# A new written order for the steps of chunk-selected attention and a gated feed-forward

## The chip, the core and the metric

The kernel runs on one core of a Trainium2 chip. Its engines are PE (matrix products), DVE (vector work), ACT (activation functions), POOL (simple tensor work, and issuing of DMAs) and SP (issuing of DMAs). Each takes its instructions from a queue of its own, strictly in the order written; they meet at semaphores. The metric is the device time of one execution in microseconds (us).

## The reference

There are 4 batches of 8 heads, with 768 positions and 64 channels per head. Attention is causal, and each query uses at most 6 key chunks of 32 positions: those with the highest upper bound of the score, which comes from each chunk's channel-wise minimum and maximum of the keys. A feed-forward follows on the 3072 x 512 result.

```python
k_min = np.min(k_chunks, axis=3); k_max = np.max(k_chunks, axis=3)
ub = sum(maximum(q * k_min, q * k_max))          # per query and chunk
top_chunks = np.argsort(where(causal, ub, -1e9))[..., -6:]
attn = softmax(where(sel & causal, scale * q @ k.T, -1e9)) @ v
xn = x / sqrt(mean(x * x) + 1e-6) * rms_g        # x: heads side by side
out = (silu(xn @ w_gate) * (xn @ w_val)) @ w_out # 512 -> 1536 -> 512
```

## The kernel before

**Tiling.** Two heads make a pair p, so there are 16 pairs, four for each batch b. A pair is prepared (place `a`), scored (place `s`) and feeds one column block of its batch's rows. The feed-forward of a batch goes in two halves of 384 rows (places `f0.0`, `f0.1`, ... ), each behind a norm (`n0.0`, ...) of three 128-row blocks.

**Steps of preparation.** kload and qload bring keys and queries by SP's queue. kT and qT turn them on PE (line 520, three 128 x 128 transposes a step), kE and qE copy them out of PSUM (helper line 290 on ACT, 294 on DVE). kmx and kmn reduce the chunks' extremes, dif subtracts them, relu takes the positive part of the queries (line 636 on ACT, 638 on DVE or POOL). ub multiplies bounds on PE (lines 737 and 795), ubE copies them out, up turns them, ubm adds the causal mask, max and sel find and mark the six best, grd guards, selT and selC (pairs 0 to 2) or a DMA transpose qX (line 560, from pair 3 on) put the marks below the queries. kC and qC cast keys and queries to bf16 (line 294 on POOL), qN lays queries out for the DMA transpose. The keys' operand, one of three sets in KE, also has constant rows: a step ke0 copies them into set 0, and two steps ke (70 and 71, lines 388 and 389, two DMAs each on SP's queue) into sets 1 and 2.

**Scores and the rest.** sc are the score products (line 882, with a causal triangle at 888 in batch 0), exp the exponentials on ACT (line 899), mask cuts the triangle on POOL in later batches (line 905), av multiplies by the values (line 918), xb divides and stores a head's columns (lines 938 and 939, DVE). The norm sums squares (sq: line 966 on ACT, 969 on DVE), eps (979), a root on POOL (987), scales rows (xs, line 995, DVE) and turns them (tp, line 1017 on PE, with an eviction tpE, in batch 0; DMA transposes xT in later batches). gate (line 1051) and val (line 1072) are four products of 384 columns each; tanh (1058, ACT), tg (1064) and hh (1080, both DVE) form the gated activation; po (line 1092) is the output product, poE its eviction, out the store (line 1107). The weights wg, wv (line 440) and wo (445) are loaded in two parts each by POOL's queue, which also loads v (line 476).

**What sets the order.** Nothing is scheduled at run time. Every unit of work is a step with a number, counted in the order in which the code adds it. PROGRAM is one long list of words: a letter for the engine (P PE, A ACT, D DVE, G POOL, S SP), the step's number, and the slots of the buffers that the step opens. `run` assigns them, and the steps are then emitted in that order, so the list fixes each engine's queue, which of two allowed engines does a step, and which slot of a pool (8 PSUM banks `ps`, 7 `nat` for loads, 3 `set`, ...) a buffer takes. A step that opens a slot waits for the last user of that slot.

```python
for word in program.split():
    n, _, slots = word[1:].partition(":")
    s = self.steps[int(n)]
    s.eng = engines[word[0]]
```

**Fillers.** Steps 4 to 51 and 290 to 328 (busy, line 339) multiply zeros into a bank that nobody reads. Only those that the list names are emitted.

**Numbers used below.** 70, 71: ke. 222, 330, 541, 470: the key loads of pairs 2, 3, 6, 5. 331, 333: pair 3's kT; 542, 544: pair 6's; 471, 473: pair 5's. 103, 239, 346, 415: relu of pairs 0, 2, 3, 4. 69: ke0. 199: the last score of pair 1 in the new list. 412: a cast of pair 4's keys; 343: one of pair 3's. 76 and 78: the two parts of wg; 77 and 79: of wv. 1260 to 1319: gates, vals and what belongs to them in `f0.0`; a gate is 1260 + 5 ht and its val three more, for the 12 blocks ht. 1335 to 1348: the second norm, with eps 1338, root 1339, xs 1340 and tp 1341.

## Time and profile before

| what | value |
|---|---|
| median of 3 runs | 312.37 us (311.37 to 313.6) |
| the profiled execution | 312.63 us |
| its span, first to last instruction | 310.9 us |
| PE, DVE, ACT, POOL busy | 300.8, 232.2, 182.2, 119.5 us |
| granted TensorE clock, mean | 0.999 |
| DMA moved | 35.35 MB |

The profile shows one execution. Busy times of PE include modelled ends of matmuls that overlap the next one; where it matters, starts are compared. "Idle before" names what ended a wait. The page's row of PE by 40 slices has 9 tenths or more in all but four slices: the first, third, seventh and last.

### The profile page before, as it was taken

The page shows a single profiled execution, that of the slowest core. Times are in us where ns is not written, and L with a number is a line of the kernel's source. Part 1 is how long each engine was busy: PE and PEld are TensorE (multiplying, and loading weights), DVE is VectorE, ACT ScalarE, POOL GpSimd, SP SyncE. Part 2 cuts the span into 40 slices and gives each one's busy share as a digit, 9 for nine tenths or more (in the row PEclk, how much of TensorE's full clock was granted, in tenths as well). Part 3 has the DMA queues.
Part 4 walks back from the last instruction along what each step waited for, and adds up shares of the span by engine and source line. Part 5 has one row for each costly group of instructions (what it writes and reads, how often), then busy time and mean ns, then how long its engine had stood idle before and what let it go on. Part 6 is the DMA issues. An engine that isn't in the chain of part 4 may idle for free.

```text
span 310.9 us, 7415 instructions
## 1 busy us (share of the span) xinstructions
PE 300.8 (97%) x2764; PEld 190.4 (61%) x2782; DVE 232.2 (75%) x651; ACT 182.2 (59%) x405; POOL 119.5 (38%) x176
## 2 busy tenths in 40 slices
PE   7989998999999999999999999999999999999995
PEld 3657875666667764667776456666665455565542
DVE  5888988998977887789987897875743764477621
ACT  5789987672588763866997336667872303433110
POOL 8588856654547840632775104514030110000000
PEclk9999999999999999999999999999999999999999
DMA  9999999999999997996237136533000055200013
GB/s 172 221 170 175 121 209 209 158 168 150 154 176 206 201 163 145 231 163 165 55 26 50 33 74 178 53 74 29 3 0 2 34 86 186 102 2 0 0 70 136
DMA packets 113300, 35.35 MB, mean 114 GB/s; under 512 B 106224, under 2 KB 110064, under 8 KB 113264
## 3 DMA queue, kind: packets, MB, share of 16 engines
q1 hardware_dynamic: 83152, 26.62, 43.0%
q0 software_dynamic: 28512, 7.87, 25.4%
q10 hardware_dynamic: 1600, 0.39, 0.6%
q8 instruction: 22, 0.36, 0.5%
q14 instruction: 14, 0.11, 0.1%
HBM read 28.57 MB, written 6.29 MB: 112 GB/s over the span
## 4 chain that ended last, share of the span: by engine, by line
PE 87%; DMA 8%; POOL 2%; ACT 1%; issue 1%; ACTq 0%; SPq 0%; POOLq 0%
PE vp L1072 20%; PE po L1092 20%; PE gp L1051 19%; PE sc L882 10%; PE av L918 6%; DMA wg<-in_moe_w_gate_dram 5%; PE pq L520 3%; PE pk L520 3%; PE ub L795 2%; DMA knat<-in_k_dram 2%; PE ub L737 1%; DMA qnat<-in_q_dram 1%; POOL ke L294 1%; PE up L817 1%; PE busy L339 1%; POOL rt L638 1%
## 5 line engine op out<-in xcount | busy, mean ns | idle before, releaser
L899 ACT ACTIVATE pt<-sc 128x512 bf16<-128x512 f32 (+1 forms) x192 | 94.0, 556 | 21.2 <-PE sc L882 18.4
L1058 ACT ACTIVATE sg<-gp 128x384 bf16<-128x384 f32 x96 | 45.7, 495 | 72.2 <-PE gp L1051 62.6
L1072 PE MATMUL vp<-xT,wv 128*128 128x384 bf16 x384 | 74.4, 326 | 1.6 <-DMA wv<-in_moe_w_val_dram 1.5
L1051 PE MATMUL gp<-xT,wg 128*128 128x384 bf16 x384 | 74.2, 326 | 0.1
L1092 PE MATMUL po<-wo,hh 128*128 128x512 bf16 x271 | 66.8, 379 | 0.7
L1064 DVE SCALAR_TENSOR_TENSOR tg<-sg,gp 128x384 bf16<-128x384 bf16 x96 | 51.9, 549 | 20.6 <-ACT sg L1058 19.2
L1080 DVE TENSOR_TENSOR hh<-vp,tg 128x384 bf16<-128x384 f32 x96 | 51.5, 552 | 18.5 <-PE vp L1072 17.7
L882 PE MATMUL sc<-qs,ke 128*128 128x128 bf16 (+4 forms) x420 | 59.3, 251 | 0.0
L1072 PEld LDWEIGHTS <-wv 128*128 128x128 bf16 x384 | 35.8, 98 | 26.4 <-DMA wv<-in_moe_w_val_dram 1.8
L1051 PEld LDWEIGHTS <-wg 128*128 128x128 bf16 x384 | 35.7, 98 | 22.5 <-DMA wg<-in_moe_w_gate_dram 0.5
L1092 PEld LDWEIGHTS <-hh 128*128 128x128 bf16 x288 | 27.5, 98 | 27.5
L918 PEld LDWEIGHTS <-pt 128*128 128x128 bf16 x672 | 34.8, 98 | 11.1 <-POOL pt L905 0.3
L918 PE MATMUL av<-vx,pt 128*128 128x65 bf16 x672 | 41.2, 193 | 0.1
L905 POOL TENSOR_SCALAR_AFFINE_SELECT pt<-pt 128x512 bf16<-128x512 bf16 (+1 forms) x48 | 24.5, 522 | 38.5 <-ACT pt L899 38.1
L882 PEld LDWEIGHTS <-ke 89*128 89x128 bf16 (+1 forms) x420 | 31.0, 97 | 10.0 <-issue 1.4
L294 POOL CAST ke<-kt 64x768 bf16<-64x768 f32 x30 | 25.3, 846 | 7.3 <-PE sc L882 2.8
L987 POOL TENSOR_TENSOR ri<-ms,mhalf 128x3 f32<-128x3 f32 x8 | 7.2, 904 | 33.6 <-DVE ms L979 33.5
L995 DVE SCALAR_TENSOR_TENSOR xs<-xb,ri,gains 128x512 bf16<-128x512 bf16 x24 | 17.2, 751 | 3.1 <-POOL ri L987 2.9
L939 DVE TENSOR_TENSOR xb<-av,rden 128x384 bf16<-128x384 f32 (+1 forms) x34 | 18.2, 534 | 1.2
L520 PE MATMUL pk<-ident_f,knat 128*128 128x128 f32 x96 | 16.0, 282 | 1.7 <-DMA knat<-in_k_dram 1.7
L476 POOL DMA_DIRECT2D vx<-in_v_dram x16 | 17.3, 1079 | 0.1
L653 DVE MAX8 m<-ubm 128x8 f32<-128x8 f32 (+4 forms) x192 | 16.8, 160 | 0.2
(91 smaller groups left out, 300.6 us busy)
## 6 DMA issues: line engine op xcount, KB each, us to landing
out_dram<-osb SPq DMA_DIRECT2D x24, 256.0 KB, 2.3
knat<-in_k_dram SPq DMA_DIRECT2D x30, 192.0 KB, 4.4
qnat<-in_q_dram SPq DMA_DIRECT2D x30, 192.0 KB, 5.1
vx<-in_v_dram POOLq DMA_DIRECT2D x16, 192.0 KB, 5.9
wg<-in_moe_w_gate_dram POOLq DMA_DIRECT2D x2, 768.0 KB, 11.7
wv<-in_moe_w_val_dram POOLq DMA_DIRECT2D x2, 768.0 KB, 10.6
...
qs<-qn SPq DMA_TRANSPOSE x26, 2.8
```

What stands on the lines that cost most here:

```text
L294: engine[e].tensor_copy(out_, in_)
L520: nc.tensor.transpose(t[:, j * P:(j + 1) * P], nat[w].tile[:, j0 + j].rearrange("p h d -> p (h d)"), ident_f[:])
L882: nc.tensor.matmul(t[:, x:x + m, :].rearrange("p a b -> p (a b)"), ke[kk, kb * P:(kb + 1) * P], qs[kk, q0 * P:(q0 + m) * P], start=not tri ...
L899: nc.scalar.activation(out=t[:, 0:nn, :], in_=sc.tile[:, 0:nn, :], func=ACT.Exp, scale=SCALE)
L905: nc.gpsimd.affine_select(out=pt.tile[:, 0:nd, :], in_=pt.tile[:, 0:nd, :], compare_op=ALU.is_ge, fill=0.0, base=0, pattern=[[0, nd], [1, ...
L918: nc.tensor.matmul(av.tile[:, qi - i0, :], pt.tile[:, x, :], VX[c.v.slot][:, hl * NT + kb, :], start=(begin and m == 0), stop=(left[0] == ...
L1051: nc.tensor.matmul(t[:], wg[:, g, hs], XT[b].tile[:, g, cols], start=(g == 0), stop=(g == NP - 1))
L1058: nc.scalar.activation(out=t[:], in_=gp.tile[:], func=ACT.Tanh, scale=0.5)
L1064: nc.vector.scalar_tensor_tensor(out=t[:], in0=sg.tile[:], scalar=1.0, in1=gp.tile[:], op0=ALU.add, op1=ALU.mult)
L1072: nc.tensor.matmul(t[:], wv[:, g, hs], XT[b].tile[:, g, cols], start=(g == 0), stop=(g == NP - 1))
L1080: nc.vector.tensor_tensor(out=t[:], in0=vp.tile[:], in1=tg.tile[:], op=ALU.mult)
L1092: nc.tensor.matmul(po.tile[:], hhs[ht].tile[:, th * P:(th + 1) * P], wo[:, ht, :], start=(ht == 0), stop=(ht == NHT - 1))
```

## The change

Only PROGRAM differs. Each of the 1878 steps of the old list is in the new one; the new list has ten more words, fillers 30 to 39 (36 fillers instead of 26). 91 steps go to their other engine: 43 from DVE to ACT, 30 from ACT to DVE, 7 from POOL to ACT, 4 from DVE to POOL, 4 from POOL to DVE and 3 from ACT to POOL. Of the relus named above, 103 goes from DVE to ACT, 346 from POOL to ACT, 239 from ACT to DVE and 415 from POOL to DVE; ke0 goes from ACT to DVE. Nearly every step's place and slots change. On SP the q and k loads keep their order, but the two ke steps, the transposes and the stores move among them: 70 now stands ahead of 222, and 71 between 222 and 330. On POOL the loads of v and of the weights keep their order; the casts, differences, guards and masks move among them.

The beginning of both lists, to the first feed-forward steps, and their ends:

```diff
@@ PROGRAM @@
 PROGRAM = (
-    "S83:0 S88:1 S89 S82 D3 G0 D56 D55 D53 D54 D60 G63 A2 G65 P4:0 D59 P5:1 G66 P6:2 D58 P7:3 D57 G67 P8:4 S154:2 "
-    "P9:5 G68 P86:6 S159:3 P10:7 G72 A87:0 P11:0 A69 D97:0 P92:1 D96:0 P12:2 G64 S335:4 G73 P84:3 D93:1 P90:4 A85 "
-    "P13:5 P14:7 A91 P15:6 D95 P16:0 A99:0 P17:2 G101 D94 S222:5 P157:1 P155:5 D98 G62 A158:2 D103:3 P18:3 G61 "
-    "P19:7 P20:4 S71 D156 P104:6,0 G102 D1 D52 D165:1 G168:1 P160:2 S330:6 A106:0 P162:3 D164:1 G74 A105 P21:1 "
-    "A161:4 P107:7 A163 G167 P336:4 S70 D108:0 P338:5 A171:5 P22:0 G166 D109:2 P23:6 P24:1 A100 D110 S541:0 "
-    "P172:2,3 A337:6 D112:0 A339 D111 P225:7 A173:0 D174 P113:0 G346:3 A226:1 S227:1 P175:6 A114 P223:1 D176:1 "
-    "P25:4 P26:5 D177:3 P331:2 P333:3 D178 A224 G115:0 S404:2 P119:7 D332:2 A334 P147:6 A179:1 P135:4 D340:4 "
-    "A148:0 G170 P128:5 P116:0 A136:1 D180 S399:3 P544:1 A117:2 D341:2 P150:3 P125:2 A545:0 P181:6 P141:4 A151:3 "
-    "D232:5 A126:4 P138:0 G342 G236:2 P347:1,3 A120:5 D182 A129:6 G169 P228:2 A139:7 P230:7 S546:5 G183:1 D348:0 "
-    "A349 P542:5 D229:5 A231 P350:6 D233:3 A142:8 P190:0 G345:0 P118:1 P121 A239:6 P144:3 P149:2 D351:2 P152 "
-    "P184:7 G234 G235 A191:9 D352:6 P240:4,6 D543 A145:2 G238 D353 A185:5 P215:0 P122:5 G251:2 A241:0 D242 P143 "
-    "A216:0 P146 P131:3 P243:7 A354 P405:4 A123:3 G237 D244:0 P209:6 P140 P137 A132:8 P218:0 D245:7 P193:7 A210:2 "
-    "G358:3 P407:5 D406:3 A219:7 P203:3 A194:1 D246 P133 P124 P187:6 A408 D248:0 G247 P127 A204:8 P196:0 D153:0 "
-    "P402:4 A188:3 P199:7 P217:5 P249:3 D355 A197:4 P130 P212:2 D250 S356:0 P211 A403:4 P195:6 G556:1 P206:0 "
-    "A200:0 A213:6 P186 P400:4 G555:1 D134 A207:2 P264:7 P201 S357 P286:3 P214 P277:2 A265:1 G554 D401 P189 "
-    "P258:0 P252:1 A278:5 D409:0 G343 P274:7 A259:0 S475:6 P261:4 A253:6 P205 D552:0 P192 G344 P198 P255:2 A275:3 "
-    "P271:0 G415:1 D202 A256:8 S470:1 P267:1 P279:7 P220 P208 A287:9 A268:4 P266:2 D551:1 P283:6 A272:5 P288 "
-    "P362:3 P257 P276 A262:7 P280:1 S75 D221 P269 P254 P369:0 P260 A281:2 P359:4 G412:2 D410:1 A370:1 P263 P282 "
-    "A284:9 P273 P366:5 G76 D270 A363:8 P285 A360:3 P389:1 G77 P371:0 P364:6 P386:3 D329 A367:4 P361 P373:2 "
-    "A390:6 G411 D365 G553 P368 P395:4 G78 A387:0 P471:5 D372 P416:7,1 D472:6 A1248:2,0 D1246:1 A1247:2 P379:6 "
-    "P478:3 D418:0 A396:7 P547:0 D1249:3 D417 P27:5 A374:2 G1250:4 P397:1 D548:5 P392:4 P476:7 A380:5 P382:5 "
-    "P473:2 D1251:0 A383:9 P391 P388 P376:0 A393:1 D1254:1 P375:6 P384 P1252:5 A479:2 P394 D1257:2 P381 A477 "
-    "P1255:4 P419:3 A377:8 D398 G486:0 P1258:7 A1253:0 P378 D1259 P549:0 A1256 D385 P28:1 P29:5 A474 D420:1 "
-    "P1260:7 A1336:5,0 D421:7 G413 P1280:1 A1335:1 D480:6 P1268:4 A1337:2 G414:0 D422 A1261:0 P1285:6 D1338:0 "
-    "D423 A1281:1 D424 G1339:1 P1270:5 D1262:2 A1286:3 S426 D1282:4 P1275:2 A1271:5 D1346:3 P1263:3 A1276:6 S425 "
-    "D1272:7 P1265:7 D1277:0 P1305:1 D1343:0 A1266:1 S559:0 P1288:5 D550 D1264:0 P1344:2 G557:3 P1315:0 D1287:5 "
-    "A1345 S564:4 D1267:6 P439:3 A1316:2 P449:6 D1289:1 P445:2 P1300:7 A450:3 D1269:2 P1295:5 G427:0 A440:4 "
-    "D481:2 A1301:3 P1283:6 A446:7 D1317:1 G79 A1296:5 P457:4 D1302:6 P560:3 A458:6 P436:2 G482 D1297:2 P1347:0 "
-    "G81 A561:1 P562:7 D1348 P565:4 A563 D1284:3 P428:5 P463:3 A437:0 D1340:1 P432:0 G572:0 P487:7,6 A429:2 "
-    "D570:3 A464:9 P1273:2 G451 A489:0 D488 A566:4 P1341:5 G485:0 P567:3 A1306:3 D1342 P459:6 A433:1 P490:7 "
-    "D1274:4 G430 P1364:4 D569:2 G80 P466:5 P1349:0 A467:5 D491:0 P465 P442:2 D571 D568 P1399:5 A443:8 D1307:5 "
...
-    "S1848 P1935:1 D1894:4 S1843 D1924:7 P1851 D1919:15 P1926 D1852:0 P1936 S1853 P1931 P1937 P1932 D1938:2 P1927 "
-    "S1939 D1933:1 S1934 A1928:0 S1929 "
+    "S83:0 S88:1 S89 S82 G0 D3 D59 P4:0 P5:1 A2 G65 D55 D56 P6:2 D53 D1 D60 P7:3 G66 P8:4 D54 P9:5 G61 G67 S154:2 "
+    "P86:6 P10:7 G68 P11:0 S159:3 A87:0 G74 P12:1 D69 P13:2 P92:3 G64 G62 D96:0 G63 P90:4 G72 A93:1 S335:4 P14:5 "
+    "D97:0 P84:7 A91 P15:0 P16:6 D85 A103:2 P17:1 P18:2 S70 P19:5 D95 G99:0 A101 P155:3 D94 P157:4 S222:5 D52 D58 "
+    "P20:0 G98 G100 A158:3 P104:6,7 D57 A156 G73 D164:1 S71 P160:1 A106:0 P162:2 A105 D165:1 G102 P21:5 P107:0 "
+    "A163:4 P22:4 S330:6 A161 P338:3 D108:0 G166 P336:7 G168:1 A171:5 D109:2 P23:6 P24:5 D110 P25:2 G169 A337:6 "
+    "P172:4,1 A111:0 D112 G345:0 S541:1 P113:0 A174:0 P225:6 A173 D114 P223:5 A339 P175:2 A346:0 P26:7 S227:0 "
+    "P27:1 D176:1 P141:4 A226:2 P135:3 D177:3 A224 P331:0 D178 A136:0 P150:7 P333:1 G115:0 D332:1 P138:2 A151:1 "
+    "A179:1 P122:6 D180 A334 P128:5 P144:3 G170 A139:2 P28:7 D341:2 P181:0 A123:3 S404:2 P147:1 A129:4 P29:7 "
+    "G236:2 D340:4 P30:2 A182 P31:6 P32:7 P542:5 S399:3 G342 P33:2 G167 P347:6,7 D543:5 A142:5 D233:3 G235 A148:6 "
+    "P184:2 D232:5 A349:0 P196:0 A348 P215:5 G183:1 P34:4 A145:7 P35:1 P228:7 A185:8 S546:4 P230:6 G234 A197:9 "
+    "D229:4 P193:4 P350:1 D231 P140:3 P124:2 P143 P125:7 A194:2 D239:3 G237 P407:0 A216:3 D351:2 P240:6,4 D408:6 "
+    "A126:5 G414:1 D352:6 P209:1 P149 A242:0 D241 P119:5 A210:6 D353 G251:2 P243:0 P130 P131:7 P137 D244:0 P190:4 "
+    "A132:4 P187:6 A120:0 G354 D245:7 P146 P544:1 G238 A188:7 D246 P133 P195:0 P116:7 A191:4 P402:5 D248:0 G247 "
+    "P218:6 A117:2 D355 P206:4 A403:0 P192 G344:0 P249:7 A207:4 P118 S356 P127 P203:5 D250 A219:2 P212:4 G358:3 "
+    "P121 A204:5 P152 P400:6 D134:0 A213:0 P274:7 S357 P189 P405:5 D401 A275:1 P271:4 D406 A545 P277:2 P205:6 "
+    "A272:7 D153 P186 P214 P217 P286:7 P283:1 A278:5 P264:5 D415:2 P258:4 A284:8 P280:3 D410:0 P199:2 A287:0 "
+    "P273:1 S475:5 A200:3 G412:1 P198 P285 P261:7 A281:7 D552:1 P201 P288 P211 P252:2 G343 A259:9 P276 P255:3 "
+    "D551:0 A265:8 S470:6 P366:4 A262:3 P359:5 D409:1 A253:0 P282 P279 P386:7 S75 A367:6 D329 P260:2 P208 P220 "
+    "A256:1 P266 P369:4 G76 D202 A387:7 P379:1 P382:3 P257 A370:5 G411 D221 P362:7 G77 A360:9 P254 P263 P267:0 "
+    "P389:4 A268:4 P371:5 P368 A363:2 P392:6 G78 A390:8 P269 P373:0 D372 P395:7 A393:1 D270 P364:4 P361 P471:5 "
+    "A380:0 P549:6 D365 A383:3 P473:2 P478:1 A396:5 D1246:2,0 P376:4 A1248:1 P547:3 D1247:2 P476:7 A472:3 A377:6 "
+    "P397:5 D1249:3 P394 D548:4 G1250:4 A374:4 P378:4 A477:1 P416:3,0 D1251:0 D1257:1 P391 P384 P1252:7 A418:0 "
+    "P381 A417 P388 D1254:2 P1258:0 A1253:0 P375 P419:3 D398 A479 P1255:7 A1259 D385 P36:1 P37:5 A1256 D420:1 "
+    "P38:1 D550 A1335:5,0 P1280:0 D421:7 A1337:1 D1336:2 P1285:4 D422 P1275:5 A1286:0 D1338:6 D424 P1265:3 A423 "
+    "G1339:1 A1281:1 D1287:2 S426 A1276:3 P1270:1 D1282:4 A1266:5 P1288:7 D1340:3 A486:6 S425 P1260:6 D1343:0 "
+    "A1271:6 A474 P1341:4 D1346:1 P1263:0 A557:2 G483:2 D1272:7 P1268:2 A1342 D1267:0 S559:0 A1261:1 G413 P1344:1 "
+    "D1289:0 P1315:4 D1345 G484 P1305:3 D1277:6 A1316:5 S564:1 D1262:2 P1347:7 G554:0 P1300:1 D1317:3 A1348 "
+    "G556:0 D1269:1 P445:5 P457:6 A1306:1 P1283:4 D1264:2 A458:2 G553 G427:0 P463:7 A446:9 P428:2 D1284:3 P436:0 "
+    "P460:6 A429:5 D481:2 P560:5 G79 A461:1 P432:4 P1349:2 D1307:5 A437:6 G485:1 D480:2 P562:6 A561:0 P567:3 "
+    "A1301:0 P1273:0 A563 D568:3 G482 G430 A1350:2 P439:5 D1302:4 P487:6,3 A433:8 G555 D1274:4 D569:3 G434 P565:1 "
+    "A489:0 P1399:4 A566 D488 D570:3 P453:0 A440:3 P490:3 A454:0 P435:6 P431 P1295:1 D1351:1 A575:5 G571 G455 "
+    "D491:0 P449:5 G81 P459:0 A1296:0 D492:4 P577:2,3 A464:7 D493 A1400:7 D494 A450:4 D495 P456 P1278:7 A578:0 "
+    "S496 G451 A582 P39:5 G80 D1279:5 P583:2 D1297:2 P1379:3 S497 D1401:6 P441 P447 P579:5 D584:2 A1380:0 D585:1 "
+    "P1303:7 D581 D580 P438 P466:1 P442:4 D586:5 P1364:2 A467:8 D592:7 A443:5 G573:1 D1381:7 P1298:5 D1304:6 "
+    "G574:1 P1310:1 D1299:7 P1402:4 D593 A1311:0 P524:3 D594 D595 P503:7 P468 P1367:5 A525:2 D1403:8 S597 A504:0 "
+    "D1312:4 P452 P507:3 P520:4 A1365:2 P462 P528:7 A508:3 P1318:1 D1366:6 S596 A521:9 D587 P1290:3 A529:6 "
...
+    "D1869:10 P1898:5 P1935:6 D1899:13 D1838:17 P1844:4 D1909:19 P1925:1 P1845 P1903:5 P1930:7 D1904:21 P1846 "
+    "P1926 A1847:0 P1849:0 S1848 P1927 P1931 A1928:1 P1679 P1932 D1680:2 P1936 S1681 D1933:0 P1850 S1934 S1929 "
+    "P1841 P1937 D1842:2 P1851 S1843 A1938:0 S1939 A1852:1 S1853 "
 )
```

176 rows, old and new, of the table PROGRAM are left out of this document.

## The prediction

> **What bounds the kernel now.** I read the page's head first, then busy time by stretch, then the chain of waits.
>
> ```profile
> span 310.9 us, 7415 instructions
> PE 300.8 (97%) x2764; PEld 190.4 (61%) x2782; DVE 232.2 (75%) x651; ACT 182.2 (59%) x405; POOL 119.5 (38%) x176
> ```
> ```profile
> 0.00:17.60 17.60, 15.75 (x126) 9.20 (x128) 12.56 (x50) 11.97 (x22) 12.85 (x29) 1.00 1.10 198
> 17.60:49.00 31.40, 29.42 (x448) 22.71 (x447) 27.88 (x82) 28.74 (x68) 22.70 (x28) 1.00 1.29 169
> 49.00:62.00 13.00, 11.48 (x79) 7.02 (x78) 11.43 (x34) 8.83 (x22) 8.41 (x9) 1.00 1.17 178
> 62.00:180.00 118.00, 117.58 (x1201) 78.21 (x1208) 99.92 (x282) 78.09 (x178) 58.49 (x87) 1.00 0.91 139
> 180.00:300.00 120.00, 119.58 (x887) 70.18 (x893) 76.83 (x202) 54.02 (x117) 17.06 (x26) 1.00 0.24 52
> ```
> ```profile
> 56.87 0.65 PE vp L1072 x4
> 301.31 5.79 PE po L1092 x26
> 307.13 0.60 ACT osb L292
> ```
>
> A row of the second fence gives the stretch, its length, and busy us with counts for PE, PEld, DVE, ACT and POOL, then the granted clock, DMA share and GB/s. From 62 to 300 PE is idle 118.00 - 117.58 + 120.00 - 119.58 = 0.84 us. Nothing is to be won there unless work is taken away, and an order takes none away. The end is PE's last product at 301.31 + 5.79 = 307.10, one eviction of 0.60 and the last store, and both orders end so. A new order can win before 62, and can lose anywhere.
>
> Busy time flatters PE there, since ends are modelled. I use starts instead: four 384-column products take 0.65 us on the chain.
>
> ```profile
> 16.96 0.84 PE L520 MATMUL pk<-ident_f,knat 128*128 128x128 f32 x6
> 20.75 0.52 PE L520 MATMUL pk<-ident_f,knat 128*128 128x128 f32 x3 [1.28 <-DMA knat<-in_k_dram]
> 42.09 0.52 PE L520 MATMUL pk<-ident_f,knat 128*128 128x128 f32 x3 [0.42 <-DMA knat<-in_k_dram]
> 48.51 0.59 PE L339 MATMUL busy<-zeros 128*128 128x512 bf16 x2
> 48.99 1.46 PE L1051 MATMUL gp<-xT,wg 128*128 128x384 bf16 x8
> 51.90 0.82 PE L1072 MATMUL vp<-xT,wv 128*128 128x384 bf16 x4 [1.45 <-DMA wv<-in_moe_w_val_dram]
> ```
>
> This is PE's timeline; brackets hold idle time and what ended it. The first gate starts at 48.99. Ahead of it stand 140 PE steps that compute, in the old order and, counted in the program, in the new one: the same 140. After it the same steps remain too. So the forecast is a shift of the first gate, plus what changes in the waits after it.
>
> **The change, part by part.** Loads first.
>
> ```profile
> 8.57 1.72 SPq L500 DMA_DIRECT2D knat<-in_k_dram  x2
> 10.40 0.79 SPq L388 DMA_DIRECT2D ke<-e_all  x1
> 11.24 0.59 SPq L389 DMA_DIRECT2D ke<-e_all  x1
> 11.88 1.27 SPq L500 DMA_DIRECT2D knat<-in_k_dram  x2
> 13.19 0.55 SPq L388 DMA_DIRECT2D ke<-e_all  x1
> 14.48 1.23 SPq L500 DMA_DIRECT2D knat<-in_k_dram  x2
> ```
> ```profile
> knat<-in_k_dram SPq DMA_DIRECT2D x30, 192.0 KB, 4.4
> ```
>
> SP issues pair 2's keys at 8.57, a set's constant rows (ke, two DMAs) at 10.40, pair 3's keys at 11.88, the other ke at 13.19, and the next keys at 14.48. The new order puts one ke step ahead of both pairs' keys. The q and k loads do keep their order among themselves, but these two now start later by a ke step, 14.48 - 13.19 = 1.29 us; what follows 14.48 is unmoved. Pair 3's second key DMA goes out about half way through 11.88 to 13.15, and key loads land 4.4 after issue: 16.9 before (its transposes, step pair 331 and 333, start at 16.96), 18.2 after. This is an estimate from those rows. **Step 331 starts 1.3 later.** In front of it PE is not late: the first bound matmuls come earlier, since pair 0's relu goes from DVE to ACT.
>
> From there to the first gate I compare work.
>
> ```profile
> 17.61 0.54 DVE L294 COPY kt<-pk 128x384 f32<-128x384 f32 x1
> 21.91 1.12 DVE L294 COPY qs<-st 64x768 bf16<-64x768 bf16 x2 [0.24 <-PE st L708]
> 23.50 0.42 DVE L294 COPY ubs<-ub 96x256 f32<-96x256 f32 x1 [0.47 <-PE ub L737]
> 24.17 0.56 DVE L294 COPY qt<-pq 128x384 f32<-128x384 f32 x1 [0.24 <-PE pq L520]
> 43.12 0.68 DVE L969 CUSTOM_DVE_ANT_0 junk<-xb 128x512 bf16<-128x512 bf16 x1
> 45.23 2.08 DVE L995 SCALAR_TENSOR_TENSOR xs<-xb,ri,gains 128x512 bf16<-128x512 bf16 x3
> ```
>
> - DVE, from pair 3's key copy (17.61) to the last xs of the first norm (45.23 + 2.08 = 47.31): 43 steps in both orders. It loses a selection copy, three bound copies and a key copy (1.12 + 3 x 0.42 + 0.54 = 2.92) and gains two relus, a square sum and two query copies (2 x 0.60, the relu row below, + 0.68 + 2 x 0.56 = 3.00). Nothing is won: + 0.1.
> - ACT: the counterpart swaps, level within a few tenths by the same kind of sum. It is busy 28.74 of 31.40, so it cannot take more.
> - PE: three score steps of pair 0 (512, 1024 and 128 columns with their mask) now stand before step 333: 0.7, at 0.22 for 512 columns, which the chain's 0.65 for four of 384 gives. Eleven fillers (busy, L339) stand in the stretch where there were three. The row at 48.51 has two, with the gate 0.48 behind: 0.24 each with the hand-over; eight are 1.9. They are put where PE waits, or else on the path: 0 to 1.9. Net - 0.7 to + 1.2.
> - Load waits: those of 1.28 (pair 6's keys) and 0.42 (pair 5's) go where the consumer stands later behind an unmoved load. Pair 6's first transpose now follows eight of pair 0's scores and a selection transpose, and pair 5's follows all of pair 3's scores but one: up to 1.7 back.
>
> All three engines are nearly full in this stretch, so 331's lateness isn't made up by speed, only out of those waits. The first gate comes between 48.99 + 1.3 - 0.7 - 1.7 = 47.9 and 48.99 + 1.3 + 1.2 = 51.5. DVE, the engine nearest to the norm, has the same work and also waited for PE in the old stretch (the brackets), which leaves a little to absorb. I take 49.5, a little under the middle, because fillers are likelier beside waits than on the path: **+ 0.5**.
>
> ```profile
> 9.19 0.60 DVE L638 TENSOR_SCALAR rt<-qt 128x768 f32<-128x768 f32 x1
> 9.44 1.03 POOL L294 CAST qs<-qt 64x768 bf16<-64x768 f32 x1
> 15.38 2.14 POOL L638 TENSOR_SCALAR rt<-qt 128x768 f32<-128x768 f32 x1 [2.50 <-ACT qt L290]
> 36.49 2.14 POOL L638 TENSOR_SCALAR rt<-qt 128x768 f32<-128x768 f32 x1
> 38.57 0.82 POOL L294 CAST ke<-kt 64x768 bf16<-64x768 f32 x1
> 39.34 0.82 POOL L440 DMA_DIRECT2D wg<-in_moe_w_gate_dram  x1
> 40.17 0.75 POOL L440 DMA_DIRECT2D wv<-in_moe_w_val_dram  x1
> 41.31 0.79 POOL L440 DMA_DIRECT2D wg<-in_moe_w_gate_dram  x1
> ```
>
> Weights: ahead of wg (step 76) POOL loses two relus of 2.14 and four casts of 0.82 (7.6) and gains three casts, a difference and a guard (about 3.2): 4.4 less. I cost that at nothing. Step 412, two places ahead, writes key set 1, which pair 1's last score (step 199) still reads, and 199 stands 11.5 us of PE work before the first gate: 38.0. With 412 and 343 of 0.82 each, wg goes out near 39.6, and wv, behind one difference, near 40.7, against 40.17. Counted from issue as before (40.17 to the wait's end at 51.90), wv lands near 52.4. But the new order puts five gates, not two, ahead of the first val: 49.5 + 5 x 0.65 = 52.75. **The wait of 1.45 goes**, with 0.3 to spare; if the cover fails, it returns in part: - 1.45, bounds - 0.5 and - 1.45.
>
> The Trainium skill (SBUF — State Buffer, "Who interferes with whom") has a rule against such moves: single-input copies and tensor_scalars of DVE, SBUF to SBUF, can take a port pair that POOL shares, for the whole instruction. The row at 9.44 agrees: 1.03 beside a DVE relu, against 0.82 at 38.57. Two relus and the copy of the constants now run on DVE; by the rule POOL loses some 0.2 for each, wv lands 0.6 later at 53.0, 0.25 of its wait is back, and the sum would be 312.5 instead of 312.2.
>
> Next late: the second norm's transpose (tp, step 1341) stands seven products behind the first gate, 49.5 + 7 x 0.65 = 54.05. Its xs is the twelfth DVE step after the first norm's last xs; at 0.42 to 0.69 each, by the rows above, some 6.0 us. That xs ends about 1.0 before the gate (its transpose and eviction lie between), so this one ends near 54.5, and PE's gates are queued behind tp: **+ 0.5** (0 to 1).
>
> After that the weights' second half (wv, step 79) goes out behind the second norm's root, five casts and a v load, about as late as in the old order, and its first user stands 20.7 us of PE work behind the gate instead of 19.8. From 62 on the distance in PE work from a bank's last matmul to its next is of the same kind in both orders (for scores behind exponentials the least is 0.8 against 0.9), so no wait is added: 0 to + 3.
>
> Sum against the profiled execution, 312.63: + 0.5 - 1.45 + 0.5 = **312.2**. The median of the runs shown, 312.37, is 0.26 lower, so I predict 311.9.
>
> **The rivals.**
> - *The start gets faster.* POOL's 4.4 us count after all, because 199 ends sooner, pair 3's keys land as before, and the gate starts at 48.6 or sooner, with no wait at tp. For: POOL's two relus leave just ahead of the casts. Against: DVE and ACT have no less to do. 312.63 - 0.4 - 1.45, less 0.26: 310.5; with 331 not late at all, 309.2.
> - *Slower: the late keys stay on the path.* In-order PE stands at 331 until the keys land, and the eight more fillers are paid in full. It decides once PE reaches 331 before 18.2, and no wait follows that could absorb it: gate at 51.5, then + 2.5 - 0.5 + 0.5: 314.9. For: all three engines nearly full. Against: the waits of 1.28 and 0.42, and DVE's brackets.
> - *Slower: the dense part gets holes.* It has 0.84 us of idle in 238; new neighbours on the banks, and 91 steps of the whole program on other engines, leave 2 to 5 us: 314 to 317.
> - *The clock.* The Trainium skill (TensorE: Matmul & The Clock Gate, Part 1) says that PE falls to half clock after about 3.4 us idle. The clock column here is 1.00 throughout with fillers in the waits; a halved 3 us stretch would cost 1.5, so 313.4. No single wait that I see reaches that.
>
> **How the numbers follow.** Forecast 0.46 (311.9, own range 310.5 to 313.6); faster start 0.20; late keys 0.15; holes 0.16; clock 0.03. One per cent, 3.1 us, is about what runs of this kernel (311.37 to 313.6) can tell from no change. Faster by more needs under 309.3: half of the first rival and a rest of the forecast, 0.11. Slower needs over 315.5: most of the holes (0.14), a third of the late keys and a rest, 0.21. Within: 0.68. The range, 309.4 to 316.2, leaves out about one in ten at the fast end and as much at the slow one; it covers the bounds of the gate (47.9 to 51.5) and two thirds of the holes.
>
> **What would show it.** Step 331 near 18.2; pk waits at 20.75 and 42.09 gone; first gate 49 to 50; no wait of vp for wv; a short wait of PE at tp; PE idle under 2 us from 62 on. Wrong if the gate moves by over 2 us, if vp still waits, or if PE shows new waits on ACT or DVE past 62.

## The result, and the profile after

The new order takes **336.06 us** (median of 6 runs, 334.71 to 336.69) against 312.21 (6 runs, 311.26 to 313.6): a ratio of 1.076, with a 95% interval of 1.073 to 1.080. The forecast of 311.9, within one per cent, was wrong, and so was its range, which ended at 316.2. The profiled execution took 336.17, its span 334.3. In some kernels below a few executions take longer than the rest; a ratio is of those within 1.5% of the kernel's fastest.

Head and clock row of the page of the new kernel:

```profile
span 334.3 us, 7455 instructions
PE 309.3 (93%) x2792; PEld 195.0 (58%) x2792; DVE 228.5 (68%) x640; ACT 189.1 (57%) x420; POOL 110.8 (33%) x172
PEclk9999985999759999999999999999999999999999
```

Two dips of the granted clock are new, in the sixth and seventh slice and in the eleventh and twelfth. The same stretches as before, in the same columns (start and end, length, busy us of PE, PEld, DVE, ACT and POOL with counts, clock, DMA share, GB/s):

```profile
0.00:17.60 17.60, 16.04 (x128) 9.53 (x128) 12.80 (x49) 11.06 (x23) 14.54 (x32) 1.00 1.15 199
17.60:49.00 31.40, 25.22 (x360) 18.81 (x360) 24.37 (x72) 25.59 (x57) 15.02 (x22) 0.98 1.21 155
49.00:62.00 13.00, 9.37 (x97) 7.49 (x98) 4.93 (x17) 5.25 (x13) 0.28 (x1) 0.66 0.56 110
62.00:180.00 118.00, 109.84 (x1075) 72.98 (x1073) 90.75 (x261) 79.59 (x180) 55.75 (x84) 0.96 0.96 142
180.00:300.00 120.00, 118.51 (x979) 70.85 (x977) 81.43 (x217) 61.77 (x138) 25.18 (x35) 1.00 0.34 58
```

In the second and third row PE, DVE, ACT and POOL all do less than before: none of them is the bottleneck, all wait. From 62 to 300 PE is idle 8.16 + 1.49 = 9.65 us instead of 0.84. PE's timeline says at which tiles (brackets: idle time and what ended it):

```profile
18.45 0.52 PE L520 MATMUL pk<-ident_f,knat 128*128 128x128 f32 x3 [1.18 <-DMA knat<-in_k_dram]
41.14 0.38 PE L882 MATMUL sc<-qs,ke 128*128 128x128 bf16 x4 [1.80 <-DMA qs<-qn]
52.47 0.88 PE L520 MATMUL pk<-ident_f,knat 128*128 128x128 f32 x3 [6.69 <-DMA knat<-in_k_dram]
61.36 3.41 PE L1051 MATMUL gp<-xT,wg 128*128 128x384 bf16 x20 [0.16 <-ACT xT L290]
94.12 1.03 PE L882 MATMUL sc<-qs,ke 128*128 128x128 bf16 x8 [7.83 <-DMA qs<-qn]
222.51 0.40 PE L882 MATMUL sc<-qs,ke 89*128 89x128 bf16 x4 [1.49 <-DMA qs<-qn]
```

**First hole.** The first gate starts at 61.36 instead of 48.99. PE idles 6.69 for pair 5's keys, then works at half clock: 0.66 in the stretch of 13 means half clock for 8.8 us, to 57.8, of which PE has work from 52.47 on, 5.3 us, and so loses 2.7. The waits of 1.18 (pair 3's keys) and 1.80 (pair 3's transposes) ahead of it are the new order's too, those of 1.28 and 0.42 were the old one's: that makes 10.7 of the 12.37 by which the gate moved; no row assigns the other 1.7. **Second hole.** It idles 7.83 for pair 5's transposed queries, with about 2.35 lost to the clock behind it. The sum, those 12.37 for the gate, less the 1.45 for wv that val no longer waits, plus 7.83, 2.35 and 1.49 at 222.51, is 22.6 of the 23.4 by which the span grew.

Both times a small transfer comes late. Before, the second key DMA of pair 5, pair 5's transposes and the two halves of wo went out so:

```profile
37.04 1.27 SPq L500 DMA_DIRECT2D knat<-in_k_dram  x2
76.33 2.56 SPq L560 DMA_TRANSPOSE qs<-qn  x2
61.15 0.88 POOL L445 DMA_DIRECT2D wo<-in_moe_w_out_dram  x1
66.04 0.84 POOL L445 DMA_DIRECT2D wo<-in_moe_w_out_dram  x1
```

After, SP's and POOL's queues, and two pieces of the chain of waits (start, us). The row of four transposes merges pair 5's, out at 79.93 and 81.59 and done by 83.69, with two of pair 6's, out only from 95.52 on:

```profile
36.42 4.14 SPq L500 DMA_DIRECT2D knat<-in_k_dram  x2
79.93 19.10 SPq L560 DMA_TRANSPOSE qs<-qn  x4
```
```profile
32.99 1.08 POOL L476 DMA_DIRECT2D vx<-in_v_dram  x1
39.14 0.75 POOL L440 DMA_DIRECT2D wg<-in_moe_w_gate_dram  x1
41.19 0.79 POOL L440 DMA_DIRECT2D wv<-in_moe_w_val_dram  x1 [0.20 <-issue]
77.99 0.88 POOL L445 DMA_DIRECT2D wo<-in_moe_w_out_dram  x1
80.71 0.84 POOL L445 DMA_DIRECT2D wo<-in_moe_w_out_dram  x1
```
```profile
39.06 13.27 DMA knat<-in_k_dram
81.59 12.48 DMA qs<-qn
```

The second key DMA of pair 5 goes out at 39.06, wg at 39.14. It takes 13.27 to land where the old order's took 4.3 (issued at 37.66, with wg at 39.34). Pair 5's transposes go out between two halves of wo and land 10.0 and 12.5 after issue; in the old order they took 2.8 and 2.5, as the second half of wo landed within 1 us of their issue. What the DMA engines did from 43.3 to 47 of the new kernel (queue; packets, MB, share of 16 engines' time):

```profile
q0 software_dynamic: 456, 0.68, 100.1%
q1 hardware_dynamic: 311, 0.08, 15.9%
```

q0 carries POOL's weights, q1 SP's keys. Packets come from both, three of q0 to two of q1, but those of q0 hold 1.5 KB and those of q1 256 bytes, so the keys move about a ninth of the weights' bytes. The Trainium skill (DMA: Bandwidth & Descriptors, Queues, rings and completion order) has the rule that each DMA engine goes round the queues that have work, one packet at a time; the trace agrees in kind, with 311 packets against 456 where equal turns would give equal numbers.

### The profile page after: what moved, and what is told of

Its sections match the earlier page's. It is cut to its first block, busy times and chain, and to the rows that moved or that the text cites. A ratio compares the mean times of both kernels' runs of the same rounds, so it can differ in the third digit from the quotient of the medians.

```text
span 334.3 us, 7455 instructions
## 1 busy us (share of the span) xinstructions
PE 309.3 (93%) x2792; PEld 195.0 (58%) x2792; DVE 228.5 (68%) x640; ACT 189.1 (57%) x420; POOL 110.8 (33%) x172
## 4 chain that ended last, share of the span: by engine, by line
PE 75%; DMA 14%; SPq 5%; ACT 2%; DVE 1%; issue 1%; POOL 1%; ACTq 0%; DVEq 0%; POOLq 0%
PE po L1092 18%; PE vp L1072 17%; PE gp L1051 17%; PE sc L882 9%; DMA qs<-qn 7%; DMA knat<-in_k_dram 6%; PE av L918 5%; SPq L500 3%; PE pq L520 3%; PE pk L520 3%; PE ub L795 2%; SPq L560 1%; DMA qnat<-in_q_dram 1%; PE ub L737 1%; PE up L817 1%
## 5 line engine op out<-in xcount | busy, mean ns | idle before, releaser
L899 ACT ACTIVATE pt<-sc 128x512 bf16<-128x512 f32 (+3 forms) x192 | 94.8, 551 | 39.0 <-PE sc L882 32.4
L1072 PE MATMUL vp<-xT,wv 128*128 128x384 bf16 x384 | 75.8, 329 | 0.0
L882 PE MATMUL sc<-qs,ke 128*128 128x128 bf16 (+5 forms) x420 | 59.6, 255 | 11.3 <-DMA qs<-qn 11.3
L1092 PE MATMUL po<-wo,hh 128*128 128x512 bf16 x288 | 69.2, 379 | 0.0
L1072 PEld LDWEIGHTS <-wv 128*128 128x128 bf16 x384 | 36.4, 99 | 23.4 <-issue 1.6
L882 PEld LDWEIGHTS <-ke 128*128 128x128 bf16 (+1 forms) x420 | 31.3, 99 | 23.4 <-DMA qs<-qn 10.8
L1092 PEld LDWEIGHTS <-hh 128*128 128x128 bf16 x288 | 27.4, 98 | 27.3
L918 PE MATMUL av<-vx,pt 128*128 128x65 bf16 x672 | 39.5, 195 | 0.0
L294 POOL CAST ke<-kt 64x768 bf16<-64x768 f32 x32 | 26.4, 833 | 24.7 <-PE sc L882 12.1
L292 ACT ACTIVATE osb<-po 128x512 f32<-128x512 f32 x13 | 7.8, 596 | 33.0 <-PE po L1092 33.0
L294 POOL CAST qn<-qnat 128x768 bf16<-128x768 f32 x13 | 11.2, 859 | 22.1 <-DMA qs<-qn 22.0
L520 PEld LDWEIGHTS pk<-ident_f,knat 128*128 128x128 f32 x96 | 11.7, 148 | 10.8 <-issue 8.3
```

The costliest lines, as they stand in the source:

```text
L294: engine[e].tensor_copy(out_, in_)
L520: nc.tensor.transpose(t[:, j * P:(j + 1) * P], nat[w].tile[:, j0 + j].rearrange("p h d -> p (h d)"), ident_f[:])
L882: nc.tensor.matmul(t[:, x:x + m, :].rearrange("p a b -> p (a b)"), ke[kk, kb * P:(kb + 1) * P], qs[kk, q0 * P:(q0 + m) * P], start=not tri ...
L899: nc.scalar.activation(out=t[:, 0:nn, :], in_=sc.tile[:, 0:nn, :], func=ACT.Exp, scale=SCALE)
L918: nc.tensor.matmul(av.tile[:, qi - i0, :], pt.tile[:, x, :], VX[c.v.slot][:, hl * NT + kb, :], start=(begin and m == 0), stop=(left[0] == ...
L1072: nc.tensor.matmul(t[:], wv[:, g, hs], XT[b].tile[:, g, cols], start=(g == 0), stop=(g == NP - 1))
```

## The experiments

The theory after the result: **bulk loads that overlap small transfers make both holes**. Rivals: the compute order itself lacks cover there, or the small transfers are slow for their own sake. In the diffs a line is a queue, with step numbers in order.

### The first hole

`e1_keys_early`:
```diff
 SP: 546
+475 470
 356 357
-475 470
 75
```


> The new order with pair 5's query and key loads (steps 475, 470) moved on SP's queue from behind pair 3's two DMA transposes to ahead of them; nothing else moves. Theory, late behind the weights: in the new kernel the second key DMA of pair 5 goes out at 39.06 beside wg (39.14) and wv (41.19) and lands only at 52.33, so that PE idles 6.69 us and then works at half clock to about 57.8 (a loss of about 2.7). With the loads ahead, they go out near 25 to 28 and land by 32; no wait at pair 5's first transpose, clock 1.00 there, first gate 61.4 - 6.9 - 2.7 = 51.8, time about 336.1 - 9.5 = 326.5 (325 to 328). Rival, the order of the compute steps is what is late there: PE stops a little further on for DVE, ACT or the transposes, first gate later than 57, time 331 or more.

Measured: 326.51 (ratio 1.043, 1.038 to 1.047). No wait at pair 5's transposes, the first gate at 51.66; the second hole is as it was. The theory's 326.5 and 51.8 hold. This row and the gate's of PE's timeline:

```profile
51.66 3.41 PE L1051 MATMUL gp<-xT,wg 128*128 128x384 bf16 x20 [0.17 <-ACT xT L290]
84.30 1.03 PE L882 MATMUL sc<-qs,ke 128*128 128x128 bf16 x8 [7.70 <-DMA qs<-qn]
```

`e15_weights_2us_later` leaves SP alone and moves the weights:
```diff
 POOL: 343
+411
 76
-411
 77 78
```


> The new order with one edit: the difference 411, which waits for DVE until 40.7, now stands ahead of the first wg load (76) on POOL's queue instead of behind it, so that wg goes out near 41.0 instead of 39.14 (wv and the rest of wg stay within 0.6). Pair 5's keys go out as before, the second one at 39.06. Theory, it is the overlap of these two transfers: with wg starting 1.9 later the key load is through first, lands by 44 to 46, no wait over 1 at the key transpose, first gate 51 to 53, time 326.5 to 329. Rival, the key load was stuck behind the transposes and the v load for its own sake: lands at 50 or later, 334 or more.

Measured: 328.09 over four executions, three of them from 327.08 to 329.09 (1.048, 1.044 to 1.053). The key DMA, out at 38.85 as before, lands 5.1 after issue instead of 13.27, and the hole is gone: wg, moved by 1.84, decides it. The profiled execution is the fourth, 336.72; only landings and the missing wait are read from it. POOL's row:

```profile
40.98 0.80 POOL L440 DMA_DIRECT2D wg<-in_moe_w_gate_dram  x1 [0.20 <-issue]
```

`e4_before_weights_ahead`, the cause alone in the old order:
```diff
 POOL: 344
+76 77
 415 412
-76 77
 411
```


> The kernel before with one edit: the first loads of wg and wv (steps 76, 77) moved on POOL's queue ahead of a relu and a cast (415, 412), from 39.34 and 40.17 to about 36.5 and 37.3. Nothing else moves. Theory, the order of transfers is the cause by itself: pair 5's query and key loads (35.82 to 38.31) are now in transfer together with the weights, their keys land at 45 to 51 instead of 41.95, PE idles at the key transpose and drops to half clock, first gate 53 to 57: time 316 to 321. Rival, a bulk load beside small ones costs them little, and the new kernel's hole comes from the order of the compute steps: keys by 43, first gate at 49, and val's wait of 1.45 for wv gone: 311.

Measured: 327.15 (1.044, 1.040 to 1.049): the hole appears, and is more than twice what the new order has. The sign is the theory's; the size was guessed too low (316 to 321). SP's and PE's rows; SP itself is held 10.96 for two key DMAs:

```profile
36.71 10.96 SPq L500 DMA_DIRECT2D knat<-in_k_dram  x2
```
```profile
55.06 0.87 PE L520 MATMUL pk<-ident_f,knat 128*128 128x128 f32 x3 [14.20 <-DMA knat<-in_k_dram]
```

Why were the keys late on SP's queue in the first place, 39.06 and not 37.66? `e6_v_load_early`:
```diff
 POOL: 251
+358
 354 238 247 344
-358
 412
```


> The new order with pair 3's v load (358) moved on POOL's queue from 32.99, between pair 3's two transposes, to right behind pair 2's v load at 28.4, near its place in the old order (29.38). Theory, this load is why the keys came to stand beside the weights: the second transpose landed 7.1 after issue instead of 4.5 and held SP's queue, and the key DMA behind it went out at 39.06 instead of 37.66. With the v load gone from there the transposes land by 38, pair 5's keys go out by 38 and land by 43.5, and the first hole goes: 326.5 (325 to 329). Rival, the keys are late wherever the weights go out within 2 us of them: keys at 50 or later, 334 or more.

Measured: 325.94 (1.043, 1.039 to 1.047), first gate at 50.94. SP's key DMAs now take 1.41 to go out and are done by 38.72; the second one, 1.1 us ahead of wg (37.90 and 39.01), lands 4.1 after issue:

```profile
37.31 1.41 SPq L500 DMA_DIRECT2D knat<-in_k_dram  x2
```

So the v load's place is what delays the keys in the new order. But `e11_before_v_late` makes the same move the other way in the old order:
```diff
 POOL: 251 237
-358
 247 556
+358
 555
```


> The kernel before with one edit: pair 3's v load (358) on POOL's queue from 29.38 to behind a cast of pair 6 (556), about 32.0, so that it is in transfer beside pair 3's two transposes (32.47, 33.83), as in the new order. No weight, no key and no compute step moves. Theory, this one move is what starts the new kernel's first hole: the second transpose lands near 41 instead of 38.3, pair 5's second key DMA goes out near 39.5 beside wg (39.34) and lands at 48 to 52 instead of 41.95; PE idles 6 to 9 and loses 2.5 to the clock, val's wait of 1.45 goes: 312.5 + 7 + 2.5 - 1.5 = 320.5 (317 to 323). Rival, the old order of the rest takes it up: within 1 of 312.5.

Measured: 313.35 (1.003, 1.000 to 1.005). The theory fell: the second transpose landed 5.6 after issue, where it took 7.1 in the new order, the keys went out by 38.6 and PE waited as ever:

```profile
42.33 0.52 PE L520 MATMUL pk<-ident_f,knat 128*128 128x128 f32 x3 [0.42 <-DMA knat<-in_k_dram]
```

A v load beside the transposes isn't enough. What in the new order's timing lets it hold SP's queue for 1.4 us more stays open. That the overlap with wg then makes the hole is shown by `e15_weights_2us_later` and `e4_before_weights_ahead`.

### The second hole

`e3_wo_early`:
```diff
 POOL: 78
+81 80
 1250
...
 455
-81
 451
-80
```


> The new order with the two loads of wo (steps 81, 80) moved on POOL's queue from behind the masks of pair 4 to right behind the second load of wg (step 78), where POOL has nothing to do; they go out near 42.7 and 43.5 and follow wg in the DMA queue until about 66. Theory, pair 5's transposes (79.93 to 83.69) land at 89.9 and 94.1 only because wo's 768 KB loads (77.99 and 80.71) share the DMA engines with them: they now land within 5 us of issue, the wait of 7.83 goes and with it the half clock behind it (2.35): time 336.1 - 10.2 = 325.9 (324 to 328); the wait of 6.69 ahead of the first gate stays. Rival, the transposes are slow for their own sake (four behind one another on one queue) or their marks come late: the wait stays over 4 us, time 331 or more.

Measured: 327.31 (1.048, 1.043 to 1.052). The wait of 7.83 and its dip of the clock are gone, as the theory has it. It missed a wait that the hole had covered, 2.04 at 95.97 for pair 9's keys, which stand on SP behind two transposes, and the 3.4 us at half clock that follow. Pair 5's transposes, out at 79.36 and 80.63, now land 2.7 and 2.6 after issue. No run made this hole in the old order.

`e5_both_holes`, `e9_both_mended_again` and `e14_bulk_in_gaps` mend both places, with the bulk loads in other places each time. First:
```diff
 SP: 546
+475 470
 356 357
-475 470
 75 426 425 559 564
+700
 496 497 597 596
-700
 POOL: 554
+427 79 81
 556 553
-427 79
 485 482 430 555 434 571 455
-81
 451
-80
 573
+80
```


> The new order with both places mended: pair 5's query and key loads ahead of pair 3's transposes, as before; wv's second half and one half of wo (79, 81), with the v load ahead of them (427), right behind a key cast of pair 6 (554); the other half of wo (80) behind a key cast of pair 7 (573), so that pair 5's transposes meet no bulk load; pair 9's key load (700) ahead of pair 5's transposes. Theory, the transfers are all that made the new order slow in the middle: of the 326.5 with early keys the wait of 7.87 and its half clock (2.35) go, and no new one comes: 316.3 (315 to 318); the 3.8 above the kernel before are the first gate at 51.7 instead of 49.0 and waits near 210. Rival, the new order has further waits that these two covered: 319 or more.

Measured: 320.59 (1.027, 1.024 to 1.030), the rival's time. But PE again waits for a transfer, not for the compute order: pair 5's wait is gone; now pair 6's transposes, issued at 81.57 and 84.75, overlap the last half of wo (out at 75.19, landed 8.3 later) and two v loads:

```profile
91.35 0.40 PE L882 MATMUL sc<-qs,ke 128*128 128x128 bf16 x4 [2.78 <-DMA qs<-qn]
```

`e9_both_mended_again` (here and in the next run the old places of the moved steps, all further on, are not printed):
```diff
 POOL: 251
+358
 354
...
 1339
+81
 483 413 484 554
+427 79 80
 556
 SP: 475 470
+559 564
 75 426 425
+700
 496
```


> The new order, mended at both places in another way than before: pair 3's v load (358) early, as in that run; pair 7's key and query loads (559, 564) right behind pair 5's; one half of wo (81) behind the second norm's root (1339); the v load of pair 4, wv's second half and the other half of wo (427, 79, 80) behind a key cast of pair 6 (554); pair 9's key load (700) ahead of pair 5's transposes. The bulk loads so lie in stretches in which SP has nothing in transfer. Theory, only transfers: 325.9 with the early v load, less 7.96 for the wait at pair 5's transposes, 2.35 for its half clock and 1.17 for pair 9's keys: 314.5 (313 to 316.5), no wait over 1.8 left. Rival, the compute order itself lacks cover there and waits appear elsewhere: 318 or more.

Measured: 333.33 (1.068, 1.064 to 1.072). The four loads that I put ahead of the gains load (75) pushed that one behind the weights: it landed 15.3 after issue, and the norm waited for it (11.42, put down to the norm's xs). My edit built the hole again with another small load:

```profile
60.30 0.61 PE L1017 MATMUL tp<-ident_b,xs 128*128 128x128 bf16 x4 [11.42 <-DVE xs L995]
```

`e14_bulk_in_gaps` puts 75 first and one half of wo later:
```diff
 POOL: 251
+358
 354
...
 1339 483
+81
 413 484 554
+427 79 80
 556
 SP: 475 470 75
+559 564
 426 425
+700
 496
```


> The run v_load_early with the transfers of the middle rearranged: the gains load (75) and then pair 7's key and query loads (559, 564) right behind pair 5's keys (in the run both_mended_again the gains stood behind them, landed at 59.4 behind the weights, and the first norm waited 11 us for them); one half of wo (81) behind the first cast after the second root (483), pair 4's v load, wv's second half and wo's other half (427, 79, 80) behind a key cast of pair 6 (554); pair 9's key load (700) ahead of pair 5's transposes. Theory, only transfers: the waits of 7.96 and 1.17 and the half clock of 2.35 go: 314.4 (313 to 316), gate at 50.9. Rival, the compute order has waits of its own there: 318 or more.

Measured: 317.45 to 325.24 over 4 executions, too far apart for a ratio. None reaches the theory's 313 to 316, and three lie where the rival had them (318 or more); what those three wait for is not in a trace. The one profiled, the fastest (317.45), has no hole over 1.5; all waits of its middle are still for transfers:

```profile
55.01 0.82 PE L1072 MATMUL vp<-xT,wv 128*128 128x384 bf16 x4 [0.51 <-DMA wv<-in_moe_w_val_dram]
59.53 1.47 PE L1051 MATMUL gp<-xT,wg 128*128 128x384 bf16 x8 [1.31 <-DMA wg<-in_moe_w_gate_dram]
62.83 0.47 PE L882 MATMUL sc<-qs,ke 89*128 89x128 bf16 x2 [0.95 <-DMA qs<-qn]
```

317.45 less these 2.77 is 314.7. What the compute order itself costs, some 2 us, is an estimate from this one execution and takes waits as additive; it is not shown.

### The clock

`e2_fill_holes` (24 fillers ahead of step 471, 28 ahead of 524) and `e7_fewer_fillers` (12 and 13):
```diff
+P40:5 P40 P40
...
 P471:5
...
+P41:3 P41 P41
...
 P524:3
```


> The new order with 24 fillers put ahead of pair 5's first key transpose (step 471) and 28 ahead of its first score (step 524), the two places where PE idles 6.69 and 7.83 us; 0.22 each, so that 1.6 and 1.8 us of the waits stay. Both transfers are as late as before. Theory, half of what follows each wait is the clock: the granted clock stays at 1.00 and the products behind the two waits run at full rate: 5.3/2 + 4.7/2 = 5.0 us less, time 331.0 (330 to 332). Rival, behind the waits PE stands at DVE, ACT or further transfers anyway, whatever its clock: under 2 us less, 334 or more.

Measured: 337.64 (1.079, 1.074 to 1.084). A filler that repeats on one bank takes 0.43, not the 0.22 that I counted, so they ran past the transfers and the run tells nothing of the clock:

```profile
47.45 10.31 PE L339 MATMUL busy<-zeros 128*128 128x512 bf16 x24
```

> The new order with 12 fillers ahead of pair 5's first key transpose and 13 ahead of its first score. In the run with 24 and 28 each took 0.43, not 0.22, so they ran 4 to 5 us past the transfers; these take 5.2 and 5.6 and end before the transfers do (6.69 and 7.83). Theory, clock: granted clock 1.00 throughout, 2.67 + 2.35 = 5.0 less, time 331.0 (330 to 332.5). Rival, PE's rate behind the waits doesn't matter, because other engines or transfers set it: 334 or more.

Measured: 332.16 (1.065, 1.062 to 1.070), 3.9 less than the new order. At the second place the clock stays at 1.00; at the first it still falls for 3.5 us (0.92 of 22):

```profile
40.00:62.00 22.00, 19.21 (x199) 12.60 (x200) 11.83 (x44) 12.26 (x31) 2.90 (x5) 0.92 0.77 141
84.00:102.00 18.00, 14.42 (x96) 7.22 (x95) 9.79 (x31) 6.37 (x13) 5.97 (x9) 1.00 0.98 131
```

The 3.9 are not the clock's alone: in this profile the keys also land 0.9 earlier (PE starts again at 51.58 instead of 52.47). From the end of each wait on the same products are through 0.76 sooner at the first place (to the first gate, at 59.71) and 1.93 sooner at the second (94.12 to 99.05 in the new order, 91.21 to 94.21 here). That is the clock's price here, a little under the 0.96 and 2.35 that the rates give.

### The prediction's own terms

`e13_v_early_ke_fillers` starts from `e6_v_load_early`; `e10_and_ke_fillers` and `e16_bulk_ke_fillers` make the same edit to `e9_both_mended_again` and `e14_bulk_in_gaps`:
```diff
 SP: 335
-70
 222
-71
+70
 330
+71
 541
 PE: fillers 29 to 38 left out
```


> The run v_load_early (325.9, first gate at 50.94) with two more edits: ke steps 70 and 71 behind the key loads 222 and 330, as in the old order, and fillers 29 to 38 left out. Theory of the prediction, late keys and fillers are on PE's path to the first gate: 331's wait of 1.06 goes and 2.2 of fillers: first gate 47.7 to 48.5, time 322.7 (322 to 324). Rival, the fillers lie beside waits and DVE or ACT set the gate: first gate at 50 or later, 325 or more.

Measured: 325.07 (1.037, 1.031 to 1.043), first gate at 49.24. The gate comes 1.70 earlier, half of the 3.3 expected, and the median is 0.9 lower, within the scatter of the four executions each (321.65 to 325.35 here, 323.88 to 326.47 there). The second hole waits for a transfer that doesn't come earlier:

```profile
49.24 3.41 PE L1051 MATMUL gp<-xT,wg 128*128 128x384 bf16 x20 [0.80 <-ACT xT L290]
84.34 1.03 PE L882 MATMUL sc<-qs,ke 128*128 128x128 bf16 x8 [9.77 <-DMA qs<-qn]
```

The wait is 9.77 where it was 7.80 in `e6_v_load_early`, and ends at 84.34 instead of 83.67. With the gate on time, wo still goes out around the transposes (66.27 and 68.99, the transposes at 68.13 and 70.92), so this hole does not come from the late gate.

> The run both_mended_again with two more edits: the ke steps 70 and 71 behind the key loads 222 and 330, as in the old order, and fillers 29 to 38 left out. Theory of the prediction, late keys and fillers on the path: 331's wait of 1.1 goes, and ten fillers of 0.22 no longer stand in front of the first gate: 3.3 less than that run, 311.2 (310.5 to 312.5), first gate at 48. Rival, both lie beside waits for ACT and DVE, which set the gate: less than 1 gained, first gate at 50 or later, 313.5 or more.

Measured: 331.29 (1.060, 1.055 to 1.064), 2.0 less than `e9_both_mended_again`; with the norm late for its gains, the gate at 62.01 tells nothing.

> The two runs together: v load early, transfers rearranged, ke steps back behind the keys, fillers 29 to 38 left out. Theory, the effects add: 325.9 - 11.5 - 3.2 = 311.2 (310 to 313), so that the new compute order with mended transfers is no slower than the kernel before. Rival, they don't add, as a gate that comes sooner meets its weights or the bulk loads: 314 or more.

Measured: 321.92 (1.031, 1.027 to 1.034). The parts don't add up. The earlier start brings pair 4's transposes into the queue while pair 7's loads still fight with the weights:

```profile
58.09 1.47 PE L1051 MATMUL gp<-xT,wg 128*128 128x384 bf16 x8 [1.42 <-DMA wg<-in_moe_w_gate_dram]
65.92 0.71 PE L882 MATMUL sc<-qs,ke 89*128 89x128 bf16 x2 [5.48 <-DMA qs<-qn]
```

### Can small moves make the old order faster?

`e8_before_keys_early` is `e4_before_weights_ahead` and, besides,
```diff
 SP: 546
+475 470
 356 357
-475 470
 75
```

> The kernel before with the weights ahead as in the earlier run (76, 77 ahead of the relu 415, out near 36.5 and 37.3), and pair 5's query and key loads (475, 470) ahead of pair 3's transposes, so that they are through before the weights start. Theory, the 14 us that the first of these edits cost came from the keys being behind the weights and from nothing else: the wait at pair 5's key transpose goes wholly (0.42 in the kernel before), wv lands about 3 earlier, so val's wait of 1.45 goes too: 312.5 - 0.4 - 1.4 = 310.7 (310 to 312). Rival, early weights also hold up pair 3's transposes (to 38.3) and v: a wait of over 2 us in their place, 314 or more.

Measured: 312.39 over ten executions that spread from 310.69 to 322.31 (0.997, 0.995 to 1.000). Six of the ten lie at 313.3 or below, five of them at 310.7 to 311.5, where the theory put it; the other four, from 316.6 on, are not in the ratio. The profiled one, at 321.1, shows the rival: the second transpose, issued 0.3 ahead of wg, takes 11.4. That the other slow ones have this wait, and the quick ones not, is likely but not in a trace.

```profile
46.86 0.37 PE L882 MATMUL sc<-qs,ke 128*128 128x128 bf16 x2 [8.11 <-DMA qs<-qn]
```

`e12_before_small_moves`:
```diff
 SP: 330
-70
 541
+70
 227 404 399 546
+475 470
 356 357
-475 470
 75
 POOL: 415
+76 77
 412
-76 77
 411
```


> The kernel before with small moves of DMAs alone, each with an ample margin: pair 5's query and key loads ahead of pair 3's transposes; wg and wv (76, 77) ahead of the cast 412, 0.8 earlier; the ke step 70 behind pair 6's key load (541), which goes out 1.3 earlier. Theory, each takes the wait that it aims at: 1.28 (pair 6's keys), 0.42 (pair 5's keys) and 0.8 of val's 1.45, together 2.5: 310.0 (309.5 to 311). Rival, DVE and ACT are as late as PE in this stretch, and the first two waits only move to them: 0.8 or less, 311.7 to 312.5.

Measured: 312.2 (0.999, 0.996 to 1.002). The time is the rival's, the reason isn't: PE gets ahead, and not DVE or ACT but a wait of 1.96 at 38.05 for pair 3's transposes takes it back.

`e17_before_one_ke` has the first hunk only, and `e18_before_ke_v` adds the second:
```diff
 SP: 330
-70
 541
+70
 227
```
```diff
 POOL: 237
-358
 247 556 555 554 343 344
+358
 415
```

> The kernel before with one edit: the ke step 70 behind pair 6's key load (541) on SP's queue instead of ahead of it; that load goes out 1.3 earlier. Theory, in the old order a small load that is on the path is worth its lead: the wait of 1.28 for pair 6's keys goes and the first gate comes at 47.7: 311.2 (310.7 to 311.8). Rival, pair 3's transposes, which land at 38.3 whatever PE does, take it up, as in the run before_small_moves (a wait of 2.12 there): 312.3 plus or minus 0.5.

Measured: 312.67 (1.000, 0.998 to 1.003), the rival's time, but pair 3's transposes take nothing up. The gate comes at 47.45, as the theory has it, but finds the weights still in transfer; the last row's releaser had long been done, and the second load of wg landed 0.04 ahead of it:

```profile
47.45 1.46 PE L1051 MATMUL gp<-xT,wg 128*128 128x384 bf16 x8
49.77 0.82 PE L1072 MATMUL vp<-xT,wv 128*128 128x384 bf16 x4 [0.86 <-DMA wv<-in_moe_w_val_dram]
54.84 0.82 PE L1051 MATMUL gp<-xT,wg 128*128 128x384 bf16 x4 [1.00 <-DVE qt L294]
```

> The same with pair 3's v load (358) behind a cast of pair 3 (344) on POOL's queue, from 29.4 to about 35, when both transposes are issued, so that they have the DMA engines to themselves. Theory, transposes without v in transfer land 3 to 4 after issue, near 36, so that the lead of PE at 38 is kept: 310.7 (310 to 311.5). Rival, v itself is then late for the first products with pair 3's values near 42, or runs into pair 5's keys and these into the weights: 313 or more.

Measured: 313.8 (1.003, 1.001 to 1.005). The rival: v is late, PE waits 1.62 for it at 41.12.

No version beats both kernels for certain.

## Why the prediction was wrong, step by step

- **"Load waits: those of 1.28 (pair 6's keys) and 0.42 (pair 5's) go where the consumer stands later behind an unmoved load."** This is the step that failed first. Pair 6's wait went. Pair 5's load is unmoved in the list, but its landing isn't: 52.33 by issue and chain (39.06 + 13.27). I had its issue time, wg's and the load of 4.4 in rows, and never asked what lies in transfer beside it. The lead over wg was 39.34 - 37.66 = 1.7 us in the old order and is 0.08 in the new one. The wait of 0.42 became 6.69. Moving wg by 1.84, the keys or the v load removes the hole; putting wg ahead in the old order makes one. Pair 3's transposes beside the v load, also without a term, add the 1.80 at 41.14.
- **The v loads and wo have no term in the sum.** "POOL loses two relus and four casts" was worked out for wg alone, and wg came as said (39.14 against 39.6, wv at 41.19 against 40.7, landed at 52.07 against 52.4). But 358 moved by 3.6 us (32.99 against 29.38), and wo, behind masks and casts on POOL, by 17 and 15 (77.99 and 80.71 against 61.15 and 66.04). Counted from each order's first gate that is 4.5 and 2.3 later, while pair 5's transposes go out 8.8 earlier (18.6 us behind the gate instead of 27.3): most of their meeting comes from the transposes, which the prediction never placed. The part followed the loads of q, k, wg and wv, and left out v, wo and the transposes.
- **"So no wait is added: 0 to + 3."** Wrong: 7.83 and 1.49. For the second no run was made; its transpose went out at 217.41, 0.5 behind a v load, and took 5.05 to land. I measured cover as distances of PSUM banks in PE work, which says nothing of transposes that SP issues. The bank argument itself holds: none of the new waits past 62 is on ACT or DVE.
- **The clock, "no single wait that I see reaches that", 0.03.** Its price follows from the steps before: 2.7 + 2.35. But its condition was wrong as well: waits of 2.04 and 2.78 also brought half clock (see the end).
- **331 1.3 later, at 18.2; fillers 0 to 1.9.** Right in kind: 18.45, with a wait of 1.18. Back in place and without ten fillers the gate is 1.70 earlier. With early v the gate is at 50.94 (taken 49.5, bounds 47.9 to 51.5), so these two were nearer to their upper end than "fillers are likelier beside waits" had it; no run parts the one from the other.
- **Val's wait of 1.45 goes**: yes in the first gates of the new kernel, but by luck: the gate was 12 late. In `e14_bulk_in_gaps`, with the gate at 51.08, 0.51 of it is back.
- **Second norm's tp + 0.5**: no such wait is in the profile after; with the gate so late the run can't tell.
- **The rivals.** "Late keys" had the right kind, small loads that PE meets in order, with the wrong pair and a price of 2.5; "holes" the right stretch with the wrong engines. Neither had contention on the DMA engines. Without both holes the order stands near 314.7 by the estimate above, where "late keys" had 314.9; that the two are close is luck, as its price came from other terms.
